# Block sums in parallel generators, a reordered first output group and new planner settings in an attention + two-MLP kernel

## The chip, the cores and the metric

The kernel runs on one core of a Trainium2 chip. The metric is the device time of one execution in microseconds (us). Three runs of the kernel before gave 1195.59, 1196.14 and 1196.61 us; their median, 1196.14 us, is the time that the changed kernel is held against.

## What is computed

The reference has three parts, one after the other (4 batches, 12 heads, 448 rows, 64 columns per head; all inputs of the two MLPs are double precision, the arithmetic on the chip is done in pairs of rounded fp32 parts):

```python
scores = cap * np.tanh(q @ k.T / sqrt(64) / cap)          # per batch and head
attn = softmax(scores);  x = attn @ v                     # -> x: 1792 x 768
y = (sigmoid(x @ w_gate) * (x @ w_val)) @ w_out           # 768 -> 1536 -> 768
h = y @ w_in2;  out = (h * cos(h)) @ w_out2               # 768 -> 2048 -> 768
```

## The kernel before, in words

**Who decides the order.** The program writes no fixed order of instructions. Every piece of work is a Python generator ("thread") that yields one operation at a time, and a planner (`Order`, L132 to L211) picks among the waiting operations the one with the smallest planned start time plus a penalty (`pen`), where a thread that has waited loses 0.1 us of penalty per us (L202). Planned times come from cost formulas written in the file (L214 to L230). The pick is then issued for good: each engine runs its instructions strictly in the order in which the planner picked them. A penalty thus says who goes first when two operations could start at about the same time; a negative one goes ahead of everything. A thread can also yield a condition, and is passed over until it holds. Operations marked `either` (L332) go to GpSimd (POOL) or VectorE (DVE), whichever the planner expects to end first.

**Stages.** The 1792 rows are done in two halves (`hf` 0 and 1), 896 rows each. `whole()` (L1694) is the thread that feeds TensorE (PE) after attention. Its stages, with the times at which the trace shows them: attention until 237 us; A0, gate and value of half 0 with plain three-part products (L715); B0, the product with w_out for half 0 (`result`, L1005); A1, gate and value of half 1 (`gate_value_pairs`, L1000) from 474.6 us; B1, `result` for half 1, from 638 us; then `cosine` (L1296) twice, first for half 1 (from 732.8 us), then for half 0. In `cosine` there are eight steps "C" (products of y with w_in2, two tiles of 128 features each, `pair_products`) and four steps "D" (products with w_out2, `out_group`, four feature tiles each, called a group), in the order C0 C1 C2 D0 C3 C4 D1 C5 C6 C7 D2 D3. A *stage entry* below is the time around a change of stage, when the operands of the new stage are still being made.

**Seven products for eight.** A1 and C use sums: the left and right operands are cut in two by two blocks, seven sums or differences of blocks are formed on either side, and seven products replace eight (L727). Weight sums are made by `sums` (L649). Blocks of x or y are made by `block_sums` (L1072): for each of three block rows j, blocks 1, 2 and 3 are copies, blocks 6, 5, 7 and 4 are differences formed by VectorE (`tt`, L1079). Each block is split into a high part (a ScalarE copy, L1059) and a low part (a subtraction on POOL or VectorE, L1065). It is all one thread: a difference is not formed before the block ahead of it has got its tile and its copy has been issued. The first pair of products of a stage runs by block rows (L799), so that row j is needed first; block 4 and then block 3 of a row come last (L800).

**After the products.** `pair_sums` (L814, penalty `S_PEN` = 0) adds the seven products on VectorE (L827) into two feature tiles and frees the PSUM banks; there are 8 banks. In A1 the tiles become g = gate times value (L904), and `g_split` (L925, penalty 1.0) splits them into high and low parts (L945 ScalarE, L948) for B1. In C each of them becomes h cos h by `hidden` (L1142, penalty `H_PEN` = 0.4): eight operations, ScalarE L1171, L1176, L1188 and L1193, VectorE L1179 and L1190, and the low part L1196.

**Output groups.** `out_group` (L1218) runs, for each of two column halves `nb`, over 7 row tiles t and, inside, over the group's four feature tiles kk: 3 matmuls each (L1255), one PSUM bank for each t. When the four are done, `out_evict` moves the bank to an accumulator (a ScalarE copy L1274 in the first group, a VectorE addition L1278 in the others).

**Background.** `bg_loads` and `bg` (L570, L579) load the 32 pieces of w_in2 and w_out2, convert them from double precision (per piece two ScalarE operations, L427 and L428, and four VectorE ones, L431, L439, L447, L455) and put them back in DRAM. Piece n may be loaded once the planned PE time is past 240 + 15.5 n us (`bg_go`, L595), with at most two loaded pieces waiting (`BG_RAW`). The thread that converts has penalty 1.0.

**Room.** SBUF has 49 "mid" tiles and 5 "big" ones. The pairs `W_A0` to `W_CD` (L345) give, by stage, how many mid tiles are kept for weights at least, and how many weights may take at most (`get`, `get_w`). `x_room` and `g_room` (L916, L921) hold back tiles for the split g; `G_SPARE` is added to the latter. `BG_ROOM` holds tiles back for the background.

Of the kernel before, what the change touches and what calls it, by code (L numbers as in the profile page):

```python
# [233 lines left out]
def softcap_attention_gated_mlp_cos_mlp(  # L234
# [14 lines left out]
    nc = tc.nc  # L249
    B, H, S, D = q.shape  # L250
# [15 lines left out]
    Y_ORDER = (0, 3, 1, 4, 2, 5)  # L266
    NMID, NBIG = 49, 5
    F_AHEAD = 2
    H_PEN, S_PEN = 0.4, 0.0
    LEAD, AHEAD = 99, 4  # L270
    BG_PEN, BG_RAW, BG_ROOM = 1.0, 2, 2
    BG_FROM, BG_STEP = 240.0, 15.5
    W_PEN, W_FROM = 0.3, 12
    ATT_PEN, A_PEN = 0.0, 1.0
    G_SPARE = 1, 6

    const = ctx.enter_context(tc.tile_pool(name="const", bufs=1))
    dram = ctx.enter_context(tc.tile_pool(name="dram", bufs=1, space=bass.MemoryType.DRAM))
# [63 lines left out]
    def dma(size, fn, r, w):  # L342
        return Op([("SP", 0.06, False, fn, 0.0)], r, w, size)

    W_A0, W_B0, W_A1, W_B1, W_CD = (7, 14), (7, 14), (14, 18), (8, 14), (12, 16)  # L345
    w_live = [0]

    def w_range():
# [244 lines left out]
    bg_made = [0]  # L593

    def bg_go():  # L595
        return sch.free["PE"] > BG_FROM + bg_made[0] * BG_STEP

    def bg_spare():
        return 0
# [194 lines left out]
    def pair_products(it, X, last_use, sink, by_rows=False):  # L794

        g = yield from take(1, it)
        at_bank, ready = {}, set()
        spawn(pair_sums(at_bank, ready, sink), S_PEN, "sums")
        for js in [[j] for j in range(KH)] if by_rows else [range(KH)]:  # L799
            for i in (1, 2, 6, 5, 7, 4, 3):  # L800
                if js[0] == 0:
                    if i in (1, 3):
                        at_bank[i] = ((yield from bank()), 0)
                    elif i == 2:
                        b = yield from bank(2)
                        at_bank[2], at_bank[6] = (b, 0), (b, 1)
                    elif i == 5:
                        b = yield from bank(3)
                        at_bank[4], at_bank[5], at_bank[7] = (b, 0), (b, 1), (b, 2)
                yield from product(i, *at_bank[i], g, X, js, last_use)  # L810
                if js[-1] == KH - 1:
                    ready.add(i)
# [186 lines left out]

    def gate_value_pairs(X):  # L1000
        for p in range(KF // 2):
            yield from pair_products(("pair", "g", p), X, False, GateSink(p), p == 0)
            yield from pair_products(("pair", "v", p), X, p == KF // 2 - 1, ValueSink(p))

    def result(hf, ph, order, sink):  # L1005
        for n, m in enumerate(order):
            if n == KD - 1 and hf == 0:
                done.add("again")
            pb = yield from bank(2)
            for s in range(2):  # L1010
                w = yield from take(ph, ("o", m, s))
                for kk in range(KF // 2):
                    i = s * KF // 2 + kk
                    if (hf, i) not in G:
                        yield lambda: (hf, i) in G
                    x = {kk: G[hf, i]}
                    yield from plain_product(w, x, [kk], pb, i == 0, i == KF - 1)
                    if n == KD - 1:
                        G[hf, i].free()
                w.free()  # L1020
            spawn(sink(m, pb), 0.0, "result")
# [31 lines left out]

    def block_split(X, i, j, src, o, c, room):
        t = yield from get("x", F32R, room)
        X.t[i, j] = t
        yield act(S, lambda: nc.scalar.copy(out=at(t, 0, S), in_=at(src, o, S)), [c], [t.cell("h")])  # L1059
        spawn(block_low(t, src, o, c), wpen, "blow")  # L1060

    def block_low(t, src, o, c):
        yield either(
            S,
            lambda e: e.tensor_tensor(out=at(t, S, S), in0=at(src, o, S), in1=f32(t, 0, S), op=ALU.subtract),  # L1065
            [c, t.cell("h")],
            [t.cell("l")],
            LOW_BIAS,
        )
        src.free()  # L1070

    def block_sums(X, raw, room):  # L1072

        e = {}

        def tt(dst, d0, x, x0, y, y0, r, w):
            return dve(
                S,
                lambda: nc.vector.tensor_tensor(  # L1079
                    out=at(dst, d0, S), in0=at(x, x0, S), in1=at(y, y0, S), op=ALU.subtract  # L1080
                ),
                r,
                w,
            )

        def direct(j, i):
            r, c = {1: (raw[j], 0), 2: (raw[j + KH], 0), 3: (raw[j + KH], 1)}[i]
            yield from block_split(X, i, j, r, c * S, r.cell(c), room)

        def first_sums(j):  # L1090
            r0, r1 = raw[j], raw[j + KH]
            e[j] = yield from get("t", F32, room)
            e[j].refs = 3
            t1, t2 = e[j].cell(0), e[j].cell(1)
            yield tt(e[j], 0, r0, S, r0, 0, [r0.cell(1), r0.cell(0)], [t1])
            yield tt(e[j], S, r1, S, e[j], 0, [r1.cell(1), t1], [t2])

        def later(j, i):
            r0, r1 = raw[j], raw[j + KH]
            if i == 7:  # L1100
                yield tt(r0, S, r1, S, r0, S, [r1.cell(1), r0.cell(1)], [r0.cell(1)])
                yield from block_split(X, 7, j, r0, S, r0.cell(1), room)
            elif i == 4:
                yield lambda: X.t[2, j].cell("l").ok
                yield tt(r1, 0, r1, 0, e[j], S, [r1.cell(0), e[j].cell(1)], [r1.cell(0)])
                e[j].free()
                yield from block_split(X, 4, j, r1, 0, r1.cell(0), room)
            else:
                o = {6: S, 5: 0}[i]
                yield from block_split(X, i, j, e[j], o, e[j].cell(o // S), room)  # L1110

        def steps(j):
            yield lambda: j in raw and j + KH in raw
            raw[j].refs, raw[j + KH].refs = 2, 3

        for j in range(KH):
            yield from steps(j)
            yield from direct(j, 1)
            yield from direct(j, 2)
            yield from first_sums(j)  # L1120
            for i in (6, 5, 7, 4):
                yield from later(j, i)
            yield from direct(j, 3)

# [2 lines left out]
    class HiddenSink:  # L1129
# [5 lines left out]
            return self.h[i]  # L1135

        def done(self, i):
            spawn(hidden(self.hf, 2 * self.p + i, self.h[i]), H_PEN, "hidden")

    hidden_next = [(1, 0)]  # L1140

# [76 lines left out]
    def out_group(hf, gi):  # L1218
        last = gi == KF2 // GRP - 1
        fs = range(gi * GRP, (gi + 1) * GRP)  # L1220
        for nb in range(DM // NB):
            w, ob = {}, {}

            def part(t, kk):
                f = fs[kk]
                if f % UK == 0 and f not in w:
                    w[f] = yield from take(1, ("z", f, nb))
                if t not in ob:
                    ob[t] = yield from bank()
                if (hf, f) not in Z:  # L1230
                    yield lambda: (hf, f) in Z
                z, wu, b = Z[hf, f], w[f - f % UK], ob[t]
                yield pe(
                    3 * MM384,
                    lambda: out_mm(z, wu, f % UK, t, b, kk == 0, kk == GRP - 1),
                    wu.cells() + [z[0].cell(), z[1].cell()],
                    [b.cell()],
                )

            def finish(t):  # L1240
                spawn(out_evict(hf, gi, nb, t, ob[t], last), 0.1, "out")

            for t in range(NTT):
                for kk in range(GRP):
                    yield from part(t, kk)
                finish(t)
            for wu in w.values():
                wu.free()
        for f in fs:
            for x in Z.pop((hf, f)):  # L1250
                x.free()
# [44 lines left out]
    def cosine(hf, X):  # L1296
        for kind, i in cd:
            if kind == "D":
                yield from out_group(hf, i)
                continue  # L1300
            last = i == KF2 // 2 - 1
            yield from pair_products(("pair", "i", i), X, last, HiddenSink(hf, i), i == 0)
            if last:
                done.add("y0")
# [389 lines left out]
    def whole():  # L1694
        yield from gate_value_plain(0, x0, 0)
        done.add(("A", 0))
        done.add("bg")
        X1 = Blocks()
        spawn(block_sums(X1, x1, lambda: x_room(0)), 0.8, "x1")
        yield from result(0, 0, range(KD), y_out)  # L1700
        done.add(("B", 0))
        yield from gate_value_pairs(X1)
        done.add(("A", 1))
        Y1 = Blocks()
        spawn(block_sums(Y1, y_raw[1], lambda: x_room(1)), 0.5, "y1")
        yield from result(1, 1, Y_ORDER, y_keep)
        done.add(("B", 1))
        spawn(first_y(), 0.5, "y0")
        yield from cosine(1, Y1)
        done.add("late C")  # L1710
        yield from cosine(0, Y0)
# [63 lines left out]
```

## Time and profile before

| what | value |
|---|---|
| median of three runs | 1196.14 us (1195.59 to 1196.61) |
| the profiled execution | 1195.84 us |
| its span, first to last instruction | 1194.0 us |
| mean granted TensorE clock | 0.992 of full speed |
| busy: PE, DVE, ACT, POOL | 1159.2, 913.1, 668.6, 258.6 us |
| bytes moved by DMA | 148.16 MB, mean 124 GB/s |

A profile covers one execution; its own time is 1.84 us longer than its span and 0.30 us under the median. A busy time of PE counts a matmul to the end of its modelled drain, so that short waits between matmuls are partly counted as busy; how many matmuls started in a window (the xN of a row) shows them in full.

### The profile page before, as it was taken

How to read it: one execution, taken by the hardware profiler on the slowest of the kernel's cores; microseconds unless marked ns; L12 is line 12 of the kernel's file. 1: busy time of each engine (PE TensorE's matmuls, PEld its weight loads, DVE VectorE, ACT ScalarE, POOL GpSimd, SP SyncE). 2: the span in 40 equal slices, each digit the busy share in tenths (PEclk: the TensorE clock that was granted, in tenths of full speed). 3: DMA queues.
4: the chain of work that ended last, by engine and by line, in shares of the span. 5: the costliest groups of instructions: out<-in, count | busy, mean ns of one | idle time of the engine just before them, and what ended most of it. 6: DMA issues, size and time to landing. Idle time of an engine off the chain costs nothing.

```text
span 1194.0 us, 15877 instructions
## 1 busy us (share of the span) xinstructions
PE 1159.2 (97%) x6090; PEld 989.7 (83%) x6090; DVE 913.1 (76%) x1127; ACT 668.6 (56%) x785; POOL 258.6 (22%) x140
## 2 busy tenths in 40 slices
PE   8999899999999999899998999999999998999998
PEld 4444455599999999799997998899999998999998
DVE  6999999698987876787778857837578877375862
ACT  6979788865655655433346534846356256452720
POOL 3766544400011000122211000302023312011300
PEclk9999999999999999899999999999999998999999
DMA  7424244477776775323235752203025231111303
GB/s 182 113 64 97 63 122 107 131 232 257 256 255 196 229 251 185 123 101 110 93 102 182 247 172 66 80 14 93 27 69 184 82 109 35 54 53 40 93 1 93
DMA packets 126187, 148.16 MB, mean 124 GB/s; under 512 B 49952, under 2 KB 98976, under 8 KB 126112
## 3 DMA queue, kind: packets, MB, share of 16 engines
q1 hardware_dynamic: 125824, 147.09, 39.9%
q8 instruction: 48, 0.79, 0.3%
q14 instruction: 27, 0.22, 0.1%
q10 hardware_dynamic: 288, 0.07, 0.0%
HBM read 112.13 MB, written 35.00 MB: 123 GB/s over the span
## 4 chain that ended last, share of the span: by engine, by line
PE 88%; DVE 7%; ACT 2%; issue 1%; SPq 0%; DMA 0%; DVEq 0%; ACTq 0%
PE pt L727 30%; PE pt L715 28%; PE pt L1255 19%; PE pt L1420 5%; PE pt L1395 4%; DVE r L1614 1%; ACT p L1486 1%; PE pt L1374 1%; PE pt L1441 1%; ACT p L1503 1%; DVE sum L1593 1%; DVE gl L948 1%; DVE zl L1196 1%; DVE h L827 0%; SPq L1329 0%
## 5 line engine op out<-in xcount | busy, mean ns | idle before, releaser
L727 PE MATMUL pt<-x,wh 128*128 128x448 f32 x1260 | 344.6, 369 | 7.1 <-DVE x L1065 3.7
L727 PEld LDWEIGHTS pt<-x,wh 128*128 128x128 f32 x1260 | 237.7, 189 | 31.5 <-DVE x L1065 4.4
L727 PE MATMUL pt<-x,wl 128*128 128x448 f32 x504 | 185.7, 368 | 0.0
L490 ACT CAST wh<-f 128x768 fp32r<-128x768 f32 (+1 forms) x164 | 122.9, 776 | 92.6 <-DVE f L655 50.3
L501 POOL TENSOR_TENSOR wl<-f,wh 128x768 fp32r<-128x768 f32 x41 | 80.1, 1957 | 381.8 <-ACT wh L490 297.3
L1255 PE MATMUL pt<-wh,zh 128*128 128x384 f32 x448 | 151.7, 339 | 6.1 <-ACT zh L1193 6.1
L1255 PE MATMUL pt<-wh,zl 128*128 128x384 f32 x448 | 151.9, 339 | 2.3 <-DVE zl L1196 2.3
L1255 PE MATMUL pt<-wl,zh 128*128 128x384 f32 x448 | 151.2, 337 | 0.0
L501 DVE TENSOR_TENSOR wl<-f,wh 128x768 fp32r<-128x768 f32 x95 | 96.8, 1024 | 45.9 <-ACT wh L490 45.6
L1486 ACT ACTIVATE p<-pt,tanh_scale 112x896 f32<-112x896 f32 x96 | 92.6, 1008 | 37.3 <-PE pt L1395 35.6
L727 PEld LDWEIGHTS pt<-x,wl 128*128 128x128 f32 x504 | 95.0, 188 | 9.3
L1278 DVE TENSOR_TENSOR acc<-pt,acc 128x384 f32<-128x384 f32 x84 | 46.6, 555 | 65.0 <-PE pt L1255 64.3
L1255 PEld LDWEIGHTS pt<-wh,zh 128*128 128x128 f32 x448 | 85.5, 191 | 6.8 <-ACT zh L1193 6.7
L1255 PEld LDWEIGHTS pt<-wh,zl 128*128 128x128 f32 x448 | 85.3, 190 | 3.8 <-DVE zl L1196 3.8
L1503 ACT ACTIVATE p<-p,cap_sb 112x1792 f32<-112x1792 f32 x48 | 86.2, 1795 | 0.0
L1255 PEld LDWEIGHTS pt<-wl,zh 128*128 128x128 f32 x448 | 85.4, 191 | 0.1
L715 PE MATMUL pt<-gl,wh 128*128 128x448 f32 x276 | 79.4, 369 | 4.1 <-DVE gl L948 4.1
L715 PE MATMUL pt<-xh,wh 128*128 128x448 f32 x288 | 83.4, 371 | 0.0
L715 PE MATMUL pt<-xl,wh 128*128 128x448 f32 x288 | 81.8, 365 | 0.0
L715 PE MATMUL pt<-xh,wl 128*128 128x448 f32 x288 | 81.8, 365 | 0.0
L1420 PE MATMUL pt<-p,v 112*64 112x448 f32 x384 | 77.5, 545 | 4.2 <-ACT p L1486 4.2
L1395 PEld LDWEIGHTS pt<-qs,ks 64*112 64x112 f32 x576 | 46.2, 171 | 41.9 <-ACT p L1486 16.7
(121 smaller groups left out, 2075.3 us busy)
## 6 DMA issues: line engine op xcount, KB each, us to landing
f<-kept SPq DMA_DIRECT2D x100, 384.0 KB, 3.5
kept<-f SPq DMA_DIRECT2D x36, 384.0 KB, 3.4
braw<-in_moe_w_in_dram SPq DMA_DIRECT2D x16, 768.0 KB, 5.5
kept<-bf SPq DMA_DIRECT2D x32, 384.0 KB, 2.7
braw<-in_moe_w_out_dram SPq DMA_DIRECT2D x16, 768.0 KB, 6.1
raw<-in_moe_w_gate_dram SPq DMA_DIRECT2D x12, 768.0 KB, 5.1
raw<-in_moe_w_val_dram SPq DMA_DIRECT2D x12, 768.0 KB, 5.9
raw<-in_moe_w_out_dram SPq DMA_DIRECT2D x12, 768.0 KB, 5.4
```

Of the source, the lines that this page charges most:

```text
L490: yield act(n, lambda: nc.scalar.copy(out=at(h, 0, n), in_=at(src, o, n)), sc, [h.cell("h")])
L501: lambda e: e.tensor_tensor(out=w.part(1, 0, n), in0=at(src, o, n), in1=w.part(0, 0, n).bitcast(F32), op=ALU.subtract),
L715: nc.tensor.matmul(b.ap[:, c, s0:s1], lhsT=w.part(wi, kk * P, P), rhs=x.part(xi, c * S + s0, s1 - s0), start=(first and (wi, xi) == (0, 0) ...
L727: nc.tensor.matmul(b.ap[:, c, s0:s1], lhsT=w.part(wi, o, P), rhs=x[xi][:, s0:s1], start=(first and (wi, xi) == (0, 0)), stop=(last and (wi ...
L948: lambda e: e.tensor_tensor(out=at(l, lo, n), in0=at(b), in1=f32(h, 0, n), op=ALU.subtract),
L1196: lambda e: e.tensor_tensor(out=at(zl), in0=uv, in1=f32(zh), op=ALU.subtract),
L1255: nc.tensor.matmul(b.ap[:, 0, :NB], lhsT=at(z[zi], t * P, P), rhs=w.part(wi, k * NB, NB), start=(first and (zi, wi) == (0, 0)), stop=(last ...
L1278: lambda: nc.vector.tensor_tensor(out=o, in0=ps(b, 0, NB), in1=o, op=ALU.add),
L1395: nc.tensor.matmul(ps(b, h)[:CP], lhsT=at(ks, ki * S + c * CP, CP)[r], rhs=at(qs, qi * S, S)[r], start=(n_ == 0), stop=(n_ == 2),)
L1420: nc.tensor.matmul(ps(b)[h * D : (h + 1) * D], lhsT=tv[:CP, h, c, :], rhs=at(p, (2 * j + h) * S, S)[:CP], start=(c == 0), stop=(c == NC - 1),)
L1486: lambda: nc.scalar.activation(out=two(at(p, 2 * j * S, 2 * S))[:CP], in_=both(b)[:CP], func=AF.Tanh, scale=tanh_scale[:CP],),
L1503: lambda: nc.scalar.activation(out=pv, in_=pv, func=AF.Exp, scale=cap_sb[:CP]),
```

## The change

- `block_split` holds the high copy and the low part in one thread and enters the block only after the copy has been issued. `block_sums` starts such a thread for each block (penalty `X_PEN` = 0.3) and goes on at once to the next difference. Block 4's difference waits until the low part of block 2 has been planned, noted in `low_done`, as before by its cell.
- `out_group`, for the first group and the first column half alone, runs the feature tiles 0 to 2 for all 7 row tiles first, into 7 banks, and then the fourth tile for all 7.
- A mark "entry" stops the loading of further background pieces: from the sixth of six result tiles of B0 until the second pair of A1; from the last pair of A1 until its end; from the fifth of six of B1 until C2 begins. Pieces already loaded are still converted.
- Settings: `H_PEN` 0.4 to -0.25, `S_PEN` 0 to 0.2, `BG_ROOM` 2 to 1, `G_SPARE` (1, 6) to (1, 4), `W_B0` (7, 14) to (9, 14), `W_A1` (14, 18) to (14, 16), `W_B1` (8, 14) to (7, 12), `W_CD` (12, 16) to (12, 18). `X_STEP` and `H_STEP` are 0.

```diff
-    H_PEN, S_PEN = 0.4, 0.0
+    X_PEN, X_STEP = 0.3, 0.0
+    H_PEN, S_PEN, H_STEP = -0.25, 0.2, 0.0
     LEAD, AHEAD = 99, 4
-    BG_PEN, BG_RAW, BG_ROOM = 1.0, 2, 2
+    BG_PEN, BG_RAW, BG_ROOM = 1.0, 2, 1
...
-    G_SPARE = 1, 6
+    G_SPARE = (1, 4)
...
-    W_A0, W_B0, W_A1, W_B1, W_CD = (7, 14), (7, 14), (14, 18), (8, 14), (12, 16)
+    W_A0, W_B0, W_A1, W_B1, W_CD = (7, 14), (9, 14), (14, 16), (7, 12), (12, 18)
...
     def bg_go():
-        return sch.free["PE"] > BG_FROM + bg_made[0] * BG_STEP
+        return "entry" not in done and sch.free["PE"] > BG_FROM + bg_made[0] * BG_STEP
...
     def gate_value_pairs(X):
         for p in range(KF // 2):
+            if p == 1:
+                done.discard("entry")
+            if p == KF // 2 - 1:
+                done.add("entry")
...
     def result(hf, ph, order, sink):
         for n, m in enumerate(order):
+            if n == KD - 1 - hf:
+                done.add("entry")
...
-    def block_split(X, i, j, src, o, c, room):
+    def block_split(X, i, j, src, o, c, room, low_done):
         t = yield from get("x", F32R, room)
+        yield act(S, lambda: nc.scalar.copy(out=at(t, 0, S), in_=at(src, o, S)), [c], [t.cell("h")])
         X.t[i, j] = t
-        yield act(S, lambda: nc.scalar.copy(out=at(t, 0, S), in_=at(src, o, S)), [c], [t.cell("h")])
-        spawn(block_low(t, src, o, c), wpen, "blow")
-
-    def block_low(t, src, o, c):
         yield either(
...
         src.free()
+        low_done.add((i, j))
...
             if i == 7:
                 yield tt(r0, S, r1, S, r0, S, [r1.cell(1), r0.cell(1)], [r0.cell(1)])
-                yield from block_split(X, 7, j, r0, S, r0.cell(1), room)
+                src, o = r0, S
             elif i == 4:
-                yield lambda: X.t[2, j].cell("l").ok
+                if not (2, j) in low_done:
+                    yield lambda: (2, j) in low_done
                 yield tt(r1, 0, r1, 0, e[j], S, [r1.cell(0), e[j].cell(1)], [r1.cell(0)])
                 e[j].free()
-                yield from block_split(X, 4, j, r1, 0, r1.cell(0), room)
+                src, o = r1, 0
             else:
-                o = {6: S, 5: 0}[i]
-                yield from block_split(X, i, j, e[j], o, e[j].cell(o // S), room)
+                src, o = e[j], {6: S, 5: 0}[i]
+            spawn(block_split(X, i, j, src, o, src.cell(o // S), room, low_done), X_PEN + X_STEP * j, "x")
...
         for j in range(KH):
             yield from steps(j)
-            yield from direct(j, 1)
-            yield from direct(j, 2)
+            for i in (1, 2):
+                spawn(direct(j, i), X_PEN + X_STEP * j, "x")
             yield from first_sums(j)
             for i in (6, 5, 7, 4):
                 yield from later(j, i)
-            yield from direct(j, 3)
+            spawn(direct(j, 3), X_PEN + X_STEP * j, "x")
...
+            late = GRP - 1 if gi == 0 and nb == 0 else 0
+            for t in range(NTT if late else 0):
+                for kk in range(late):
+                    yield from part(t, kk)
             for t in range(NTT):
-                for kk in range(GRP):
+                for kk in range(late, GRP):
                     yield from part(t, kk)
                 finish(t)
...
             last = i == KF2 // 2 - 1
+            if i == 2:
+                done.discard("entry")
             yield from pair_products(("pair", "i", i), X, last, HiddenSink(hf, i), i == 0)
...
         done.add(("A", 1))
+        done.discard("entry")
         Y1 = Blocks()
```

## Rows read from the trace of the kernel before

**Rows 1.** The page: busy us by engine (share of the span) and instructions.

```profile
PE 1159.2 (97%) x6090; PEld 989.7 (83%) x6090; DVE 913.1 (76%) x1127; ACT 668.6 (56%) x785; POOL 258.6 (22%) x140
```

**Rows 2.** Waits of PE: who waited for whom, us in total, times, longest.

```profile
PE pt L1255 <- ACT zh L1193: 6.1, 2, 3.1
...
PE pt L715 <- DVE gl L948: 4.1, 6, 2.2
PE pt L727 <- DVE x L1065: 3.7, 2, 2.2
PE pt L727 <- ACT x L1059: 3.4, 1, 3.4
...
PE pt L1255 <- DVE zl L1196: 2.3, 4, 1.0
```

**Rows 3.** Windows: length, busy (starts) of PE, PEld, DVE, ACT, POOL; clock; DMA share, GB/s.

```profile
475.00:500.00 25.00, 20.02 (x88) 17.61 (x88) 19.52 (x28) 12.39 (x19) 4.02 (x2) 0.86 0.41 142
500.00:525.00 25.00, 25.00 (x122) 22.71 (x121) 19.77 (x26) 10.09 (x15) 6.85 (x4) 1.00 0.23 83
625.00:650.00 25.00, 22.06 (x103) 18.66 (x102) 21.67 (x24) 21.27 (x26) 4.30 (x2) 1.00 0.58 187
650.00:675.00 25.00, 23.83 (x111) 20.37 (x111) 20.99 (x27) 9.39 (x11) 0.00 (x0) 1.00 0.78 263
675.00:700.00 25.00, 25.00 (x125) 23.16 (x125) 20.56 (x30) 13.26 (x19) 0.00 (x0) 1.00 0.56 193
725.00:750.00 25.00, 22.85 (x113) 20.77 (x112) 21.32 (x35) 11.24 (x20) 2.80 (x2) 1.00 0.26 88
750.00:775.00 25.00, 24.61 (x123) 22.57 (x121) 19.25 (x21) 20.96 (x26) 9.89 (x5) 1.00 0.25 80
775.00:800.00 25.00, 21.31 (x112) 20.98 (x113) 12.37 (x15) 11.97 (x19) 0.00 (x0) 0.93 0.06 16
...
1000.00:1025.00 25.00, 21.33 (x106) 20.43 (x105) 14.77 (x18) 13.56 (x19) 0.00 (x0) 0.86 0.06 17
...
1150.00:1175.00 25.00, 25.00 (x146) 25.00 (x145) 7.52 (x13) 0.00 (x0) 0.00 (x0) 1.00 0.15 42
```

**Rows 4.** Timeline of VectorE at the entry of A1: start, us, instruction.

```profile
485.44 1.09 DVE L827 TENSOR_TENSOR sg<-pt,part 128x896 f32<-128x896 f32 x1 [1.76 <-ACT wh L490]
...
488.10 0.62 DVE L1079 TENSOR_TENSOR x1r<-x1r,t 128x448 f32<-128x448 f32 x1
488.64 0.95 DVE L447 SCALAR_TENSOR_TENSOR bf<-braw,bf 128x768 int32<-128x768 int32 x1
```

**Rows 5.** VectorE groups at the entry of B1, 638 to 660 us: busy, mean ns.

```profile
L948 DVE TENSOR_TENSOR gl<-sg,gh 128x896 fp32r<-128x896 f32 x10 | 10.8, 1082 | 0.0
L447 DVE SCALAR_TENSOR_TENSOR bf<-braw,bf 128x768 int32<-128x768 int32 x3 | 2.8, 949 | 0.0
L455 DVE SCALAR_TENSOR_TENSOR bf<-bf,braw 128x768 int32<-128x768 int32 x3 | 2.8, 949 | 0.0
...
L439 DVE TENSOR_SCALAR bf<-bf 128x768 int32<-128x768 int32 x3 | 1.7, 551 | 0.0
L431 DVE TENSOR_SCALAR bf<-bf 128x768 f32<-128x768 f32 x2 | 1.1, 552 | 0.0
```

**Rows 6.** Timeline of ScalarE, VectorE and TensorE at the first D0.

```profile
768.52 0.95 ACT L1188 ACTIVATE u<-u 128x896 f32<-128x896 f32 x1
...
769.94 1.09 DVE L827 TENSOR_TENSOR part<-pt,h 128x896 f32<-128x896 f32 x1 [0.50 <-PE pt L727]
771.76 1.09 DVE L827 TENSOR_TENSOR h<-pt,part 128x896 f32<-128x896 f32 x1 [0.73 <-PE pt L727]
772.77 1.08 DVE L1190 TENSOR_TENSOR u<-h,u 128x896 f32<-128x896 f32 x1
...
777.66 0.45 PE L1255 MATMUL pt<-wh,zh 128*128 128x384 f32 x1 [3.05 <-ACT zh L1193]
```

**Rows 7.** The background tile bf: durations in ns, first and last start.

```profile
L455 DVE SCALAR_TENSOR_TENSOR bf<-bf,braw x32: 948/953/960, 268.3 to 730.9; 128x768 int32<-128x768 int32 x32
```

More of the change, by code (lines that the diff above doesn't have):

```diff
@@ L1070, in block_low @@
         src.free()
+        low_done.add((i, j))
     def block_sums(X, raw, room):
-        e = {}
+        e, low_done = {}, set()
         def tt(dst, d0, x, x0, y, y0, r, w):
@@ L1087, in direct @@
             r, c = {1: (raw[j], 0), 2: (raw[j + KH], 0), 3: (raw[j + KH], 1)}[i]
-            yield from block_split(X, i, j, r, c * S, r.cell(c), room)
+            yield from block_split(X, i, j, r, c * S, r.cell(c), room, low_done)
         def first_sums(j):
@@ L1137, in done @@
         def done(self, i):
-            spawn(hidden(self.hf, 2 * self.p + i, self.h[i]), H_PEN, "hidden")
+            spawn(hidden(self.hf, 2 * self.p + i, self.h[i]), H_PEN + H_STEP * ((2 * self.p + i) % GRP), "hidden")
     hidden_next = [(1, 0)]
```

## The prediction

> **What bounds the kernel now.** I read the page first: TensorE is busy for 97% of the span and VectorE, the next, for 76% [rows 1]. So PE's work sets the time, and a change that leaves the matmuls alone, as this one does, can only win the moments in which PE stands still or runs slowly. The list of PE's waits says who makes it stand [rows 2]: the high and low parts of z at line 1255 (6.1 and 2.3 us), the low parts of g at line 715 (4.1 us), and the blocks of x and y at line 727 (3.7 and 3.4 us). The list's other lines lie in attention, which the change does not reach: its settings act only after attention or in later stages.
>
> Idle time understates these waits, so I counted matmuls by window [rows 3] and compared each with an undisturbed one. Undisturbed, 25 us hold 122 matmuls at line 727 (0.205 us each), 125 at line 715 (0.20 us) and 146 at line 1255 (0.171 us).
> - Entry of A1, 475 to 500: 88 for 122, so 34 x 0.205 = 7.0 us lost.
> - Entry of B1, 625 to 675: 103 for about 124 and 111 for 125, so 35 x 0.20 = 7.0 us.
> - Entry of C, 725 to 750: 113 for about 124, so 2.2 us.
> - First D0, 775 to 800: 112 for 146, so 5.8 us, and 0.4 us idle just ahead of it.
> - Second D0, 1000 to 1025: 106 for about 145, so 6.7 us.
> - Two short waits in D1, which I take as 0.6 us of the 2.3 us for zl [rows 2].
>
> Together 29.7 us: **the ceiling** of any gain. Slow clock is in it: the granted clock is 0.86, 0.93 and 0.86 of full speed in the windows of A1 and the two D0 entries and 1.00 in those of B1 and C, where no single wait is longer than 2.2 us [rows 2, 3]. That is the lower of the two levels (1.2 instead of 2.4 GHz) for part of the window after a wait of 3 us or more; if such a wait goes, the slow matmuls go with it.
>
> **The change part by part.**
>
> *Entry of A1.* PE wants block 4 and then block 3 of the third row of x. Block 4's difference started at 488.10 us [rows 4], though VectorE stood idle for 1.76 us ahead of 485.44: two sums of line 827 and a weight difference had been put in front of it, and a background operation (0.95 us) went between it and its low part. The change takes out the background, lets line 827 wait a little (S_PEN 0.2), and no longer holds block 4 behind block 7's tile. Its difference still has penalty 0.8, and G's tiles must still be freed first. Between 0 and 7.0 us I take 5.0: most of the cause is named in the rows, not all.
>
> *Entry of B1.* From 638 to 660 us VectorE formed ten low parts of g, 1.08 us each, and eleven background operations, 2.8 + 2.8 + 1.7 + 1.1 = 8.4 us, were interleaved with them [rows 5]. Alone, the low parts are faster than PE uses them: one g feeds 6 matmuls, 1.2 us. With the background stopped from the last pair of A1, only already loaded pieces remain, and loading resumes at the stage's first matmul, so a new conversion comes several us later. Two tiles fewer held back (G_SPARE) and two fewer for weights (W_A1) let splits begin earlier. Bounds 0 and 7.0; I take 5.5, since the rows of the cover name 8.4 us that goes.
>
> *Entry of C.* As in A1, with blocks of y: bounds 0 and 2.2, I take 1.2, being half. W_B1's lower maximum (12 weights) could make the weight sums late instead; that is why not more.
>
> *D0, twice.* Here the rows show a planner's choice. The sine of h for one of the last two tiles of the group was issued at 768.52 (0.95 us), but its product (line 1190) ran at 772.77, behind two sums of line 827 for which VectorE itself waited 0.50 and 0.73 us [rows 6]. H_PEN -0.25 against S_PEN 0.2 reverses that, so the third tile comes some 3 us sooner. The sums that now go second hold banks for at most two operations longer, 2 x 1.08 us, while tile t needs a new bank only every 3 x 3 x 0.171 = 1.5 us, and one bank is free from the start. The fourth tile, taken last, is first needed after 7 x 9 x 0.171 = 10.8 us instead of 1.5 us, which no wait in the list comes near. Seven evictions then come 0.5 us apart on ScalarE in place of 2.1 us; a free eighth bank covers the first of them. Of 5.8 + 0.4 + 6.7 = 12.9 us I take 10.5; the low end is 3, if only the fourth tile's share goes. D1's 0.6 us should go as well, by the same priority.
>
> *What is given back.* Stopped pieces are converted later. All 32 are done by 731 us before [rows 7]; the third pause starts some 27 us before C and ends at C2, so two or three pieces, plus what the earlier pauses left over, move into C2 to D0. A piece costs VectorE 0.55 + 0.55 + 0.95 + 0.95 = 3.0 us [rows 5]; three cost 9.0 us of an engine that has 5.75 us of 25 free from 750 to 775 [rows 3]. The bounds on PE are 0 and 9.0; with the last penalty of all I take 1.0. New orders elsewhere make small new waits, from nothing up to the 2.2 us of one misplaced pair of operations: 2.0. The smaller BG_ROOM and the other W settings I cost at nothing, because PE shows no wait in B0, A1 or the later C steps for them to end or lengthen; if that cover went, a wait for weights would show at line 727.
>
> **The sum.** 5.0 + 5.5 + 1.2 + 10.5 + 0.6 - 1.0 - 2.0 = 19.8 us less. The profiled execution of 1195.84 us becomes 1176.0; the median is 0.3 us above it, so **1176.3 us**.
>
> **The rivals.**
> - *Room is the bound.* x's blocks and g's parts wait for tiles, not for an order, so A1, B1 and C keep their waits. For it: all are made just as the previous stage's tiles come free. Against: VectorE idles in front of block 4 [rows 4]. Only D remains, 11.1 less the 3.0 given back: 1188.0.
> - *The third tile stays late.* The reordered group meets the same wait at kk = 2, and 8 of the 12.9 us remain. For it: PE waited 3.05 us until 777.66 for a high part whose product had run only at 772.77 or later [rows 6], and moving the fourth tile alone does not hasten that. Against: VectorE's own waits of 0.50 and 0.73 us ahead of it, in which it could have run. Then D gives 4.9 instead of 10.5: 1181.9.
> - *Weights late* (slower). `hidden` now goes ahead of the weight sums too, whose penalties are 0 and 0.3. If in each of the 16 pairs of C two of its VectorE operations stand before the weights that PE needs next, that is 16 x 2 x 1.08 = 34.6 us: 1210.9. It decides once more than nine pairs are hit. Against: VectorE has 5.75 us free per 25 us, about two pairs [rows 3], and a pair's weights are made a pair ahead.
> - *The clock at the bank changes* (slower). In the reordered block PE goes to another bank after nine matmuls and later after three. If that alone let the clock fall to its lower level, its 84 matmuls would take 84 x 0.171 = 14.4 us more, 28.7 us in both: 1205.0. The trace speaks against it: the by-row pair from 733 us changes banks after every three matmuls, and its window (725 to 750) has clock 1.00 [rows 3].
> - *Nothing happens:* the waits only move, within 2.4 us of 1196.1.
>
> The Trainium skill, on its page "TensorE: Matmul & The Clock Gate", section "A second HAM failure mode: psum-queue depth-cycling", reports a kernel whose PE idled briefly while cycling through PSUM banks, so that the clock fell and rose again and again. By that, the fourth rival would hold; this trace does not bear it out.
>
> **How the numbers follow.** My forecast has 0.66 (its own range 1169 to 1184), room 0.13, the third tile 0.09, late weights 0.06, the clock 0.02, nothing 0.04. No change means within 0.2%, 2.4 us, about what measurements of this kernel can tell. Faster: 0.66 + 0.13 + 0.09 = 0.88; same 0.04; slower 0.08. The ceiling is 1196.1 - 29.7 = 1166.4. The range runs from 1168, nearly all of it won, to 1191, which holds the two partial cases with their 3 us of unknown costs; outside lie the last three cases and a little of the others.
>
> **What would show it.** Right: 120 or more matmuls in the 25 us from the entry of A1 and no clock below 1.00 there; line 948's wait under 1.5 us in total; no wait of 3 us at line 1255; line 1190 ahead of line 827 before D0; no background operation between the low parts of g; the last of the line 455 conversions after C2 begins. Wrong: waits for wh or wl at line 727 in C, waits for banks (line 1274) at line 1255, or the waits for x and gl with their old lengths.

## The result, and the profile after

The changed kernel takes 1167.65 us in the median of four runs (1165.98 to 1168.34); the kernel before, run beside it, 1196.38 us (four runs). The ratio is 0.9756, with a 95% interval of 0.9739 to 0.9773: 28.7 us less. The forecast was 1176.3 us, in a range from 1168 to 1191. So it was faster, as forecast, and by more than the range held: the median is 0.35 us below its low end.

The line of the page on busy times in the changed kernel:

```profile
PE 1148.7 (98%) x6090; PEld 983.9 (84%) x6090; DVE 922.1 (79%) x1120; ACT 670.2 (57%) x785; POOL 272.1 (23%) x147
```

The same 6090 matmuls as in [rows 1], in a span of 1166.3 us instead of 1194.0. Lines below the edit have moved: 715 is now 716, 727 is 728, 1255 is 1265, 827 is 828, 948 is 949, 1190 is 1196, 1193 is 1199, 1196 is 1202, 1059 is 1065, 1065 is 1069.

PE's waits in the changed kernel that lie behind attention, from the list of who waited for whom (us in total, times, longest):

```profile
PE pt L716 <- DVE gl L949: 0.8, 2, 0.4
...
PE pt L1265 <- DVE zl L1202: 0.5, 1, 0.5
```

These two lines, 1.3 us, are all that is left of the 19.6 us in [rows 2]. The waits for x at line 727 and for zh at line 1255 have no successor at all.

The 25 us windows of the changed kernel, in the columns of [rows 3]:

```profile
475.00:500.00 25.00, 25.00 (x124) 22.95 (x123) 20.16 (x30) 15.36 (x23) 8.84 (x5) 1.00 0.51 176
500.00:525.00 25.00, 25.00 (x125) 23.16 (x125) 22.96 (x29) 9.61 (x14) 5.96 (x4) 1.00 0.34 111
...
625.00:650.00 25.00, 24.22 (x112) 20.15 (x111) 23.74 (x29) 13.14 (x16) 2.30 (x2) 1.00 0.64 201
650.00:675.00 25.00, 25.00 (x123) 22.71 (x122) 21.74 (x32) 12.97 (x19) 0.00 (x0) 1.00 0.69 247
675.00:700.00 25.00, 25.00 (x123) 22.71 (x122) 14.19 (x23) 10.63 (x15) 0.00 (x0) 1.00 0.38 127
...
725.00:750.00 25.00, 25.00 (x123) 22.71 (x122) 19.42 (x23) 16.18 (x21) 8.47 (x4) 1.00 0.42 143
750.00:775.00 25.00, 25.00 (x138) 24.17 (x137) 22.49 (x25) 21.28 (x28) 1.98 (x1) 1.00 0.15 48
...
975.00:1000.00 25.00, 24.52 (x138) 23.76 (x137) 17.22 (x18) 15.35 (x22) 3.92 (x2) 1.00 0.06 17
```

The entry of A1 holds 124 matmul starts where it held 88, and the granted clock is 1.00 there and at both D0 entries (750 to 775 and 975 to 1000), where it was 0.86, 0.93 and 0.86 [rows 3]. Only the entry of B1 still shows a loss (112 starts of about 124). Two windows differ in a way that no wait explains: from 500 to 525 the changed kernel starts 125 matmuls against 122, from 675 to 700 it starts 123 against 125, all at clock 1.00.

VectorE ahead of the first D0 of the changed kernel, and PE's first matmul of that group (timeline: start, us, instruction). The products of the first and second tile come first, those of the third and fourth 14 us later:

```profile
740.78 2.09 DVE L1196 TENSOR_TENSOR u<-h,u 128x896 f32<-128x896 f32 x2 [1.52 <-ACT u L1194]
...
754.38 2.10 DVE L1196 TENSOR_TENSOR u<-h,u 128x896 f32<-128x896 f32 x2
756.54 2.10 DVE L1202 TENSOR_TENSOR zl<-u,zh 128x896 fp32r<-128x896 f32 x2
758.56 1.08 DVE L828 TENSOR_TENSOR h<-pt,part 128x896 f32<-128x896 f32 x1
...
758.96 0.34 PE L1265 MATMUL pt<-wh,zh 128*128 128x384 f32 x1
```

The same group's first matmul in the kernel before:

```profile
773.38 0.34 PE L1255 MATMUL pt<-wh,zh 128*128 128x384 f32 x1
```

The products (now line 1196) of the third and fourth tile stand ahead of C2's sums of line 828 and start 4.6 us ahead of the group's first matmul. Before, two of C2's sums went first, and the product at 772.77 started 0.6 us ahead of that matmul [rows 6]. The low parts of the third and fourth tile now end at 758.64, only 0.3 us ahead of the group: nobody waits, but there is little to spare.

VectorE's groups around the entry of B1 in the changed kernel, 626 to 648 us (busy us, mean ns), and the last background conversion:

```profile
L949 DVE TENSOR_TENSOR gl<-sg,gh 128x896 fp32r<-128x896 f32 x8 | 8.7, 1085 | 0.0
L456 DVE SCALAR_TENSOR_TENSOR bf<-bf,braw 128x768 int32<-128x768 int32 x3 | 2.9, 954 | 0.0
L448 DVE SCALAR_TENSOR_TENSOR bf<-braw,bf 128x768 int32<-128x768 int32 x3 | 2.9, 952 | 0.0
...
L432 DVE TENSOR_SCALAR bf<-bf 128x768 f32<-128x768 f32 x3 | 1.7, 556 | 0.2 <-ACT bf L428 0.2
L440 DVE TENSOR_SCALAR bf<-bf 128x768 int32<-128x768 int32 x2 | 1.1, 554 | 0.0
```

```profile
L456 DVE SCALAR_TENSOR_TENSOR bf<-bf,braw x32: 947/954/961, 268.4 to 779.4; 128x768 int32<-128x768 int32 x32
```

The pause did not clear VectorE at B1. Eleven background operations still stand in this stretch, as many as in [rows 5], and one still stands between any two of the low parts of g:

```profile
638.62 1.08 DVE L949 TENSOR_TENSOR gl<-sg,gh 128x896 fp32r<-128x896 f32 x1
639.62 0.95 DVE L456 SCALAR_TENSOR_TENSOR bf<-bf,braw 128x768 int32<-128x768 int32 x1
640.49 1.08 DVE L949 TENSOR_TENSOR gl<-sg,gh 128x896 fp32r<-128x896 f32 x1
```

And the last conversion now starts at 779.4 us instead of 730.9 [rows 7], some 20 us into the first D0.

### The profile page after: what moved, and what is told of

Same layout as the page of the kernel before. It is cut to its first block, busy times and chain, and to the rows that moved or that the text cites. A ratio compares the mean times of both kernels' runs of the same rounds, so it can differ in the third digit from the quotient of the medians.

```text
span 1166.3 us, 15920 instructions
## 1 busy us (share of the span) xinstructions
PE 1148.7 (98%) x6090; PEld 983.9 (84%) x6090; DVE 922.1 (79%) x1120; ACT 670.2 (57%) x785; POOL 272.1 (23%) x147
## 4 chain that ended last, share of the span: by engine, by line
PE 89%; DVE 6%; ACT 3%; issue 1%; SPq 0%; DMA 0%; DVEq 0%; ACTq 0%
PE pt L716 29%; PE pt L728 29%; PE pt L1265 20%; PE pt L1432 5%; PE pt L1407 4%; DVE r L1626 2%; PE pt L1386 1%; PE pt L1453 1%; ACT p L1498 1%; ACT p L1515 1%; DVE sum L1605 1%; SPq L1341 0%; DVE h L828 0%; DVE u L1196 0%; DVE gl L949 0%
## 5 line engine op out<-in xcount | busy, mean ns | idle before, releaser
L728 PE MATMUL pt<-x,wh 128*128 128x448 f32 x1260 | 341.0, 367 | 0.0
L502 POOL TENSOR_TENSOR wl<-f,wh 128x768 fp32r<-128x768 f32 x46 | 94.9, 2065 | 318.1 <-ACT wh L491 226.9
L502 DVE TENSOR_TENSOR wl<-f,wh 128x768 fp32r<-128x768 f32 x90 | 92.0, 1027 | 34.3 <-ACT wh L491 34.0
L1626 DVE RECIPROCAL r<-pt 128x448 f32<-128x448 f32 x24 | 70.8, 2949 | 9.3 <-PE pt L1453 9.3
```

The lines of the kernel that those rows point to most:

```text
L502: lambda e: e.tensor_tensor(out=w.part(1, 0, n), in0=at(src, o, n), in1=w.part(0, 0, n).bitcast(F32), op=ALU.subtract),
L728: nc.tensor.matmul(b.ap[:, c, s0:s1], lhsT=w.part(wi, o, P), rhs=x[xi][:, s0:s1], start=(first and (wi, xi) == (0, 0)), stop=(last and (wi ...
L1626: [("DVE", 2.95, False, lambda: nc.vector.reciprocal(out=at(r, 0, S), in_=ps(den)), 0.0)],
```

## The experiments

Each kernel was timed beside the kernel before. Four questions: what ended the waits at D0; whether the block generators and the room settings (the W settings, `G_SPARE` and `BG_ROOM`) work by themselves; what the pauses are worth; what is left at B1.

### What ended the waits at D0

**The changed kernel with the old order of the first group.**

```diff
-            late = GRP - 1 if gi == 0 and nb == 0 else 0
+            late = 0
```

> The changed kernel with the first output group in its old order (all four feature tiles of a row tile together). Theory P (the planner's penalties end the waits at D0, because they bring the third tile sooner): the time stays at 1167.6 us, within 1.5 us, and no wait over 1 us appears at the output products. Theory F (taking the fourth tile last is what ends them): a wait of some 3 us comes back at both D0 entries, and with the slow clock behind it 1173 to 1180 us.

Measured: 1167.44 us, ratio 0.9752 (0.973 to 0.9775), against 0.9756 with the new order. The same time; the only wait at the output products is 0.5 us.

**The changed kernel with the old penalties.**

```diff
-    H_PEN, S_PEN, H_STEP = -0.25, 0.2, 0.0
+    H_PEN, S_PEN, H_STEP = 0.4, 0.0, 0.0
```

> The changed kernel with H_PEN 0.4 and S_PEN 0.0 again. Theory P: both D0 entries wait as before (12.9 us lost in the kernel before), so 1178 to 1182 us, with the granted clock under 1.00 behind them. Theory F: the fourth tile taken last covers most of it, 1168 to 1171 us.

Measured: 1185.02 us, ratio 0.9897 (0.9873 to 0.992), three us more than Theory P gave. Its waits at the output products, and the window of the first D0:

```profile
PE pt L1265 <- ACT zh L1199: 7.9, 2, 5.2
...
PE pt L1265 <- DVE zl L1202: 2.2, 2, 1.8
```

```profile
750.00:775.00 25.00, 19.39 (x87) 17.71 (x86) 24.00 (x25) 20.89 (x24) 2.43 (x1) 0.86 0.11 32
```

With the fourth tile still taken last, PE waits longer for zh than the kernel before did, 5.2 us at once against 3.1 [rows 2], and the clock falls to 0.86 in that window.

**The penalties alone, in the kernel before.**

```diff
-    H_PEN, S_PEN = 0.4, 0.0
+    H_PEN, S_PEN = -0.25, 0.2
```

> The kernel before with H_PEN -0.25 and S_PEN 0.2 alone. Theory P: the D0 waits shrink from 12.9 us to some 2 us and nothing else gets better, 1184 to 1187 us. Theory F: less than 3 us gained, 1193 to 1196 us. If the penalties also reorder VectorE at the other entries, it is below 1184.

Measured: 1180.27 us, ratio 0.986 (0.9837 to 0.9883): 16 us won by two numbers. Its waits for blocks and z:

```profile
PE pt L727 <- ACT x L1059: 3.4, 1, 3.4
...
PE pt L727 <- DVE x L1065: 2.4, 2, 2.2
...
PE pt L1255 <- DVE zl L1196: 1.7, 2, 1.4
PE pt L715 <- DVE gl L948: 1.5, 4, 0.4
```

D0's waits for zh are gone, and so is the 2.2 us wait at B1 (the longest there is 0.4 us); the waits for blocks at A1 and C stay. It won more than the 10 to 12 us that Theory P gave to D0, as the third branch of the expectation had it, because the other entries moved too: 96 matmul starts for 88 in the window of A1, and 112 and 118 for 103 and 111 in the two of B1.

**The reordered group alone, in the kernel before.**

```diff
+            late = GRP - 1 if gi == 0 and nb == 0 else 0
+            for t in range(NTT if late else 0):
+                for kk in range(late):
+                    yield from part(t, kk)
             for t in range(NTT):
-                for kk in range(GRP):
+                for kk in range(late, GRP):
```

> The kernel before with the first output group taking its fourth tile last, alone. Theory P: the third tile is as late as ever and the fourth is ready right behind it, so nothing changes, 1195 to 1197.5 us. Theory F: 1184 to 1190 us.

Measured: 1197.27 us, ratio 1.0002 (0.9989 to 1.0016). Nothing. Its waits for zh and zl:

```profile
PE pt L1259 <- ACT zh L1193: 6.1, 2, 3.0
...
PE pt L1259 <- DVE zl L1196: 2.3, 4, 1.0
```

They are those of [rows 2] to a tenth. All four runs speak for Theory P: the penalties end D0's waits, and the reordering has no effect that these runs can see, with them or without.

### Blocks and room

**The changed kernel with the single block generator.**

```diff
+        spawn(block_low(t, src, o, c), wpen, "blow")
...
-            spawn(block_split(X, i, j, src, o, src.cell(o // S), room, low_done), X_PEN + X_STEP * j, "x")
+                o = {6: S, 5: 0}[i]
+                yield from block_split(X, i, j, e[j], o, e[j].cell(o // S), room)
```

> The changed kernel with the old single generator for the block sums. Theory A (each part ends its own waits and the parts add up): the waits for blocks at the entries of A1 and C come back, 7.0 + 2.2 us in the kernel before, so 1174 to 1177 us. Theory I (the parts need each other: the new room settings without the parallel generators make the blocks later than they were): a longer wait at the entry of A1 than the 5.0 us of the kernel before, 1178 us or more.

Measured: 1179.92 us, ratio 0.9856 (0.983 to 0.9882). PE waits twice for the high part of x, 5.7 us in total and 4.6 at its longest, where the kernel before had 3.4 as its longest [rows 2]. That is what Theory I said:

```profile
PE pt L728 <- ACT x L1066: 5.7, 2, 4.6
```

**The block generators alone, in the kernel before** (the diff above, the other way round; `X_PEN` 0.3).

> The kernel before with the parallel block generators (penalty 0.3) alone. Theory A: the entries of A1 and C are won, 1187 to 1190 us. Theory I: the generators take tiles from the weights under the old room settings, so a new wait appears elsewhere and less than 3 us is won in all, 1193 to 1199 us.

Measured: 1196.08 us, ratio 0.9996 (0.9977 to 1.0015). The waits for blocks are gone, and others stand in their place:

```profile
PE pt L1255 <- ACT zh L1193: 8.7, 2, 5.7
PE pt L716 <- DVE gl L949: 6.7, 5, 3.4
```

```profile
400.00:425.00 25.00, 21.60 (x92) 19.19 (x92) 21.78 (x31) 13.04 (x18) 0.00 (x0) 0.86 0.65 215
```

One wait of 3.4 us for a low part of g lies at 404 us, the entry of B0, where PE never waited before, with a clock of 0.86 behind it; the first D0 waits 5.7 instead of 3.1 us. This is Theory I again.

**The room settings alone, in the kernel before.**

```diff
-    BG_PEN, BG_RAW, BG_ROOM = 1.0, 2, 2
+    BG_PEN, BG_RAW, BG_ROOM = 1.0, 2, 1
...
-    G_SPARE = 1, 6
+    G_SPARE = 1, 4
...
-    W_A0, W_B0, W_A1, W_B1, W_CD = (7, 14), (7, 14), (14, 18), (8, 14), (12, 16)
+    W_A0, W_B0, W_A1, W_B1, W_CD = (7, 14), (9, 14), (14, 16), (7, 12), (12, 18)
```

> The kernel before with the new W settings, G_SPARE and BG_ROOM alone. Theory A: part of the entry of B1 is won, 1192 to 1195 us. Theory I: the single block generator waits longer for its tiles, nothing or less than nothing is won, 1195 to 1201 us.

Measured: 1196.95 us, ratio 1.0003 (0.9983 to 1.0023). The little that it wins at D0 and C it loses at the entry of A1, whose window now holds 73 starts instead of 88 [rows 3]:

```profile
475.00:500.00 25.00, 19.04 (x73) 14.94 (x72) 20.52 (x32) 14.00 (x22) 5.12 (x3) 0.80 0.49 157
```

**Both together, in the kernel before** (the generators and the room settings of the two runs above, with the old penalties, the old group order and no pauses).

> The kernel before with both, the parallel generators and the new room settings. Theory A: the two gains of the runs with one of them alone add up. Theory I: together they win clearly more than that sum, the waits at the entry of A1 vanish and 1184 to 1188 us results, with both D0 waits as in the kernel before.

Measured: 1181.95 us, ratio 0.987 (0.9846 to 0.9893): 15 us where the two gains by themselves add up to nothing, 2 us more than Theory I gave. The A1 entry is free and the D0 waits remain:

```profile
475.00:500.00 25.00, 25.00 (x124) 22.97 (x123) 19.67 (x30) 14.08 (x21) 7.62 (x4) 1.00 0.43 145
```

```profile
PE pt L1255 <- ACT zh L1193: 5.8, 2, 3.1
...
PE pt L1255 <- DVE zl L1196: 2.4, 2, 1.8
```

**The changed kernel with the old room settings** (the room diff above, the other way round).

> The changed kernel with the old W settings, G_SPARE and BG_ROOM. Theory A: one to three us more at the entry of B1, 1169 to 1171 us. Theory I: the parallel block generators take the tiles that weights need, and a wait of several us appears in a stage that had none, 1174 to 1178 us.

Measured: 1178.91 us, ratio 0.9836 (0.9809 to 0.9863), a little over Theory I's range. The wait at the entry of B0 is back at 404 us, 3.4 us long, as with the generators alone:

```profile
PE pt L716 <- DVE gl L949: 5.8, 6, 3.4
```

So generators with the old room make g late at B0, and the new room with a single generator makes x late at A1; each needs the other. Which of the settings it is, the least number of weight tiles in B0 (7 or 9) or another, was not tried one by one and stays open. So does the way in which the old room delays g: the runs show that it is late, and with which settings, not why.

The penalties alone won 16 us and this pair 15. Together that is 31, a little more than the 28.7 of the whole change, so little of it is left for the pauses and nothing for the reordered group.

### The pauses, and what is left at B1

**The changed kernel without pauses.**

```diff
-        return "entry" not in done and sch.free["PE"] > BG_FROM + bg_made[0] * BG_STEP
+        return sch.free["PE"] > BG_FROM + bg_made[0] * BG_STEP
```

> The changed kernel without the pauses of the background. If the pauses do what they say and cost nothing later: waits come back at the entries, the low parts of g interleaved with background operations above all, 1171 to 1175 us. If the stopped pieces cost PE time when they are made up for (the forecast's 1.0 us, up to 9.0): 1166 to 1168 us.

Measured: 1169.18 us, ratio 0.9759 (0.9726 to 0.9792), against 0.9756 with pauses. The intervals lie on each other, and the time falls between the two branches: the pauses are worth at most a few us, and stopped pieces do not cost several. The trace shows what they do at B1. Without them PE waits five times for low parts of g, 1.9 us in total, where the changed kernel waits twice, 0.8 us, and the window has 104 starts instead of 112:

```profile
625.00:650.00 25.00, 23.14 (x104) 18.57 (x103) 24.13 (x30) 14.74 (x17) 0.76 (x1) 1.00 0.45 150
```

**A lower penalty for the threads that split g.**

```diff
-            spawn(g_split(hf), 1.0, f"g{hf}")
+            spawn(g_split(hf), 0.6, f"g{hf}")
```

> The changed kernel with the penalty of the threads that split g lowered from 1.0 to 0.6. If what is left at the entry of B1 (112 matmul starts of about 124 in 625 to 650 us, some 2.4 us) is the order in which VectorE takes the low parts of g: 1164.5 to 1166.5 us. If it is the tiles or ScalarE: 1167 to 1168.5 us.

Measured: 1164.94 us, ratio 0.9719 (0.9689 to 0.9749). The time is in the branch for the order on VectorE, though the interval still touches the changed kernel's. In its profiled execution (1163.44 us) PE no longer waits at B1. Its four runs are 1163.35, 1163.44, 1166.43 and 1166.65 us, two pairs 3 us apart.

**The second pause held on through the first tile of B1.**

```diff
         for n, m in enumerate(order):
+            if n == 1 and hf == 1:
+                done.discard("entry")
...
         done.add(("A", 1))
-        done.discard("entry")
```

> The changed kernel with the second pause of the background held on through the first result tile of B1. If background operations between the low parts of g are what is left at that entry: 1164.5 to 1166.5 us. If not: 1167 to 1168.5 us.

Measured: 1163.42 us, ratio 0.9707 (0.968 to 0.9733), the fastest of all kernels here, better than the expectation, and with an interval that does not touch the changed kernel's. Its four runs lie within 0.32 us. Four of its windows:

```profile
625.00:650.00 25.00, 25.00 (x124) 22.86 (x123) 22.71 (x26) 10.65 (x13) 2.24 (x2) 1.00 0.44 134
650.00:675.00 25.00, 25.00 (x125) 23.18 (x124) 18.03 (x28) 14.63 (x20) 0.00 (x0) 1.00 0.71 237
675.00:700.00 25.00, 25.00 (x125) 23.17 (x124) 18.37 (x29) 11.76 (x18) 0.00 (x0) 1.00 0.56 185
...
725.00:750.00 25.00, 25.00 (x125) 23.18 (x124) 18.92 (x20) 19.37 (x24) 8.53 (x4) 1.00 0.48 158
```

The entry of B1 is full (124 starts against 112), and the windows behind it hold 125 starts where the changed kernel has 123. VectorE shows why. Between 626 and 648 us it still runs ten background operations, but from 633.72 on seven low parts of g stand in a row, with none between them:

```profile
633.72 1.09 DVE L949 TENSOR_TENSOR gl<-sg,gh 128x896 fp32r<-128x896 f32 x1
634.73 1.09 DVE L949 TENSOR_TENSOR g<-sg,g 128x896 fp32r<-128x896 f32 x1
635.73 5.09 DVE L949 TENSOR_TENSOR gl<-sg,gh 128x896 fp32r<-128x896 f32 x5
```

So what counts at B1 is the place of the background operations, not their number.

## Why the prediction was right and wrong

The mechanism held: PE's work is the bound, the waits at the stage entries are what can be won, and the change removes nearly all of them. Three steps failed in size. The shares taken of the waits were too small at A1, C and D0 (5.1 us in all; B1's was 1.3 us too large). The 3.0 us charged as given back did not come. And the pace of the undisturbed matmuls, taken as fixed, was not (2.2 us). Counted in the windows as the prediction did:

| step | forecast, us | measured, us | from |
|---|---|---|---|
| entry of A1 | 5.0 | 7.4 | 124 - 88 starts x 0.205 |
| entry of B1 | 5.5 | 4.2 | 112 + 123 - 103 - 111 starts x 0.20 |
| entry of C | 1.2 | 2.0 | 123 - 113 starts x 0.20 |
| both D0 | 10.5 | 12.4 | 12.9 less the 0.5 us that is left |
| D1 | 0.6 | 0.6 | no wait left |
| given back | -3.0 | 0 | no wait at 745 to 980 us |
| pace of matmuls | none | +3.0 and -0.8 | 125 for 122 starts in each of five windows from 500 to 625; 123 for 125 in each of two from 675 to 725 |
| sum | 19.8 | 28.8 | the medians give 28.7, the spans of the two traces 27.7 |

*The entries of A1, C and D0.* The steps that failed are the shares: "most of the cause is named in the rows, not all", "I take 1.2, being half", 10.5 of 12.9. Each left a remainder with no row behind it that would have to persist, and the traces show none at A1 and C and 0.5 us at D0. The working at D0 was sound: the forecast had the third tile some 3 us sooner, and counted from the group's first matmul the pair's first product is 4.0 us sooner (4.6 us ahead instead of 0.6).

*D0: for which reason.* The prediction put the gain down to the penalties and left the fourth tile's share 3 us at the low end. The four runs bear the first out; the second measured nothing. The trace agrees: the fourth tile is ready 0.3 us ahead of the group, and in the old order its first matmul comes nine matmuls, about 1.6 us, into it.

*A1 and C: a reason only half seen.* The forecast had the generators and the room as separate helps. Alone they win nothing, 0.9996 and 1.0003; together 15 us. The prediction costed "the smaller BG_ROOM and the other W settings" "at nothing, because PE shows no wait in B0": that step failed in mechanism, for with the generators and the old room a wait of 3.4 us appears at B0, and the changed kernel loses 11 us. The rival that room is the bound did not hold as it was put: with the generators alone the waits for blocks already go. Room decides whether another stage pays for it.

*B1.* Near in size (5.5 against 4.2), wrong in its cause, so the size was in part luck. The background was not cleared from VectorE, eleven operations before and after, and without pauses the time is the same within the intervals. The long wait of 2.2 us goes with the penalties alone (longest 0.4 us there) in a kernel that has no pause. That the background operations between the low parts are what is left was right all the same: in the last run, where they stand behind them, the remaining waits go.

*What is given back.* Two pieces were converted after 760 us, near the forecast, at no cost: PE waits for nothing between 745 and 980 us. "New orders elsewhere make small new waits: 2.0" found none either. The 1.0 us was picked from bounds of 0 and 9.0, the 2.0 us from bounds of 0 and 2.2; no run shows either cost in the changed kernel.

*The rivals of the other sign.* No wait for weights at line 728 appears in C. The clock did not fall at the bank changes: with the reordered group it is 1.00 in both D0 windows, and 1167.65 stands against 1167.44 us without it. The Trainium skill, page "TensorE: Matmul & The Clock Gate", section "A second HAM failure mode: psum-queue depth-cycling", tells of a kernel that cycled through PSUM banks, whose PE idled briefly between groups of matmuls and whose clock went up and down. Here PE cycles through the banks but waits only once at these products, 0.5 us, so no run here shows the idling that the page speaks of; it shows that the cycling alone left the clock at 1.00.

*The range.* Its low end, 1168, was called "nearly all of it won", while the ceiling of 29.7 us, counted from rows, put the end of the possible at 1166.4. With the charges and remainders struck out, the prediction's own terms give 7.0 + 7.0 + 2.2 + 12.9 + 0.6 = 29.7 us: that was the better forecast. But it was no ceiling. The kernel with the pause held on takes 1163.42 us, 3 us under that end. "Undisturbed, 25 us hold 122 matmuls at line 727" was read from windows that were themselves slow: the same products start 124 to 125 times in 25 us in the changed kernel's A1, and no term of the sum had that.

## What to carry to other kernels

Here the waits at A1, C and D0 came from when an in-order engine took its work, and the change won them whole, slow clock included, but for 0.5 us. So a share of such a wait needs a row that says what stays, and a guess about new waits belongs in the range, not in the sum. Where background work delays an operand, look at where it stands, not at how much of it there is: B1 came free with ten operations of eleven still there. Test settings that share a resource together: the generators and the room settings were worth nothing one by one and 15 us as a pair. And try the smallest edit first: two penalties alone gave 16 of the 28.7 us, and the reordering that looks most like the cure gave none.

## What was not expected of the hardware

Matmuls of 448 columns run at two paces at the same granted clock of 1.00: 125 starts in 25 us or 122 to 123, that is about 0.2025 or 0.2065 us from one start to the next (the timelines of 715 to 740 us, before and after). In the kernel before the slow pace begins behind the wait at A1 (122 from 500 us on) and ends behind the waits of B1 (125 from 675 us) [rows 3]; in the changed kernel A1 is fast (125) and the pace is slow behind the waits of B1 (123). The kernel with the old group order, which differs only behind 758 us, is fast there in its profiled execution:

```profile
650.00:675.00 25.00, 25.00 (x125) 23.18 (x124) 21.80 (x32) 13.05 (x20) 0.00 (x0) 1.00 0.69 245
675.00:700.00 25.00, 25.00 (x125) 23.16 (x124) 14.01 (x22) 10.62 (x15) 0.00 (x0) 1.00 0.39 127
```

That execution took 1165.94 us, the changed kernel's 1168.34, both with a granted clock of 1.00 over the whole span. By the two paces, 115 us from 643 to 758 us at the slow one cost some 2.2 us (an estimate), which is nearly all of that difference. So the pace behind the same two waits of 0.4 us can differ from execution to execution.

A wait is not needed for the change, either. In the kernel with the pause held on, PE waits for nothing from 240 to 975 us, and its products of y start 125 times in 25 us ahead of the first D0 and 123 times behind it:

```profile
850.00:875.00 25.00, 25.00 (x123) 22.71 (x121) 20.75 (x23) 19.81 (x25) 5.88 (x4) 1.00 0.41 123
```

The pairs of times 3 us apart are something else. Of the kernel with the old group order two runs took 1165.8 and 1165.9 us with a mean granted clock of 1.0, two 1168.9 us with 0.997; of the one with the lower penalty two took 1163.4 us with 1.0, two 1166.4 and 1166.7 us with 0.997 and 0.996. Three to four thousandths of the span are 3.5 to 4.7 us, so the clock covers that gap; where in those executions it fell, no trace shows. What makes the two paces stays open.
